# Moving the last eight V matmul groups of a decode attention kernel behind all transposes and scores

## The chip, the cores and the metric

The kernel runs on one core of a Trainium2 chip. The metric is device time in microseconds (us), as a median of several executions. The executions of one kernel still spread by 0.8 to 16 us, and differences of 2 us are what this study is about; so each ratio is between runs of the same rounds on the same chip, and where two kernels of different chips are set side by side, the text says so.

PE is the matmul engine (TensorE), DVE the vector engine, ACT the scalar engine; SP issues the loads. The tiles that the PE writes here (kst, sps, acc in the profiles) are in PSUM. In this kernel an engine waits for another's work, or for a load, by a semaphore.

## The reference, cut to what matters

One query token, 16 query heads of width 256, 8 key/value heads, a cache of 65,536 positions in bfloat16. For each key/value head, two query heads share it:

```
q      = x @ wq                                   # 16 heads x 256
scores = q . K^T * 256**-0.5                      # K: 8 x 65536 x 256
p      = softmax(scores)
o      = p . V                                    # V: 8 x 65536 x 256
a      = o @ wo
out    = g * a + (1 - g) * b                      # b: a small token MLP, g: a gate
```

K and V together are 537 MB, and each element is used once or twice. So the loads matter, and in this kernel the PE loads every 128x128 block of V, and of K transposed, as weights (8192 weight loads of each in the page).

## The kernel before

The cache is cut into 256 chunks of 2048 positions; a load brings four chunks of K or of V (4 MB) into one of five ring slots. I call the last loads K62, K63, V62, V63 (chunks 248 to 251 are in K62 and V62, 252 to 255 in K63 and V63). For a chunk the PE does 32 transposes of K, 32 score matmuls, one matmul that sums the probabilities (denominator) and 32 V matmuls. DVE and ACT copy the transposes out of PSUM, ACT takes the exponential.

```python
    DC = 4          # chunks per load
    NS = 5          # ring slots
    KTB = 2
    PTB = 4         # ring of probability tiles
    LAG = 2
    loads = [(w, cd) for cd in range(NCD) for w in "kv"]
    loads[-3], loads[-2] = loads[-2], loads[-3]        # ..., K62, K63, V62, V63
    # the last load comes in four pieces:
    pieces = [(0, 32), (32, 48), (48, 56), (56, 64)]
    # ... cut ...
            def load(i):                               # SP queue
                w, cd = loads[i]
                slot = i % NS
                # ... cut: wait until the slot's last user on the PE is done ...
                if i < len(loads) - 1:
                    eng.dma_start(ring[:, slot].rearrange("p n d -> p (n d)"), cache_src(w, cd)
                                  ).then_inc(sem_in[slot], 16)
                    return
                # ... cut: the pieces ...

            # PE
            def denominators(c):
                g, k = divmod(c, NCPH)
                pe.wait_ge(sem_exp, c + 1)
                if k == 0 and g >= 1:
                    pe.wait_ge(s_run, g if g >= 2 else 1)
                pe.matmul(acc[:, g % 2, DENC:DENC + 2 * NT], ones_sq[:, :], pT[:, c % PTB, :],
                          start=(k == 0), stop=(k == NCPH - 1))

            def values(c):
                g, k = divmod(c, NCPH)
                cd, cv = divmod(c, DC)
                slot, landed = slot_of("v", cd)
                if cd < NCD - 1 and cv == 0:
                    pe.wait_ge(sem_in[slot], landed)
                # ... cut: 32 matmuls, weights = V block, moving = two columns of pT ...
                ins.then_inc(sem_pv, 1)

            for s in range(NC + LAG):
                if s < NC:
                    transposes(s)
                # ... cut: the projection of q at s == 1 ...
                if 0 <= s - 1 < NC:
                    scores(s - 1)
                if 0 <= s - 2 < NC:
                    denominators(s - 2)
                if 0 <= s - LAG < NC:
                    values(s - LAG)
                # ... cut: mixer and projection of finished heads ...
            project(H - 1)

            # ACT
            def weights(c):
                act.wait_ge(sem_qk, c + 1)
                if c >= PTB:
                    act.wait_ge(sem_pv, c - PTB + 1)
                act.activation(pT[:, c % PTB, :], sps[:, c % 2, 0:2 * NT], AF.Exp, scale=scale
                               ).then_inc(sem_exp, 1)
```

The softmax here doesn't subtract the row's maximum and nothing guards it: scores larger than these inputs give would overflow.

## Time and profile before

| | before |
|---|---|
| time, median of 3 (range) | 1322.87 us (1322.7 to 1323.07) |
| span of the profiled execution | 1319.0 us (its time was 1320.84 us, 2 us under the median) |
| cache bytes, mean rate | 544 MB, 415 GB/s |
| PE busy | 1130.7 us (86%) |

The last line becomes important later: 197 packets brought 3.23 MB of instructions.

The timeline of the PE in before, at the gap that the change is aimed at (start, duration, then line, operation, tiles, count; in brackets the idle time before it and what ended it). `kst<-ident,ring` are the transposes of K, `sps<-qT,ktT` the scores, `acc<-pT,ones_sq` the denominator, `acc<-pT,ring` the V matmuls:

```profile
1282.94 2.37 PE L259 MATMUL kst<-ident,ring 128*128 128x128 bf16 x22 [0.55 <-issue]
1285.10 1.04 PE L275 MATMUL sps<-qT,ktT 128*128 128x2 bf16 x32
1286.00 0.19 PE L286 MATMUL acc<-pT,ones_sq 128*128 128x32 bf16 x1
1292.10 1.02 PE L303 MATMUL acc<-pT,ring 128*128 128x2 bf16 x32 [5.91 <-DMA ring<-in_A_v_cache_dram]
1292.98 3.57 PE L259 MATMUL kst<-ident,ring 128*128 128x128 bf16 x32
```

The PE has done transposes up to chunk 250 and comes to the V matmuls of chunk 248, whose data (V62) has not landed. It sits idle for 5.9 us, although K63, loaded ahead of V62, should be there at about 1280 us (an estimate: it was issued at 1249.4 us, and a load of K takes 29.9 us in the median).

The chain of waits of before, in order of time (start, length, what):

```profile
1261.21 30.84 DMA ring<-in_A_v_cache_dram
1292.05 0.04 issue
1292.10 1.02 PE acc L303 x32
1293.11 3.44 PE kst L259 x32
...
1301.59 1.81 PE kst L259 x32
1303.40 0.78 PE sps L275 x32
...
1313.50 0.82 PE acc L303 x32
```

From V62's landing to the last V matmul there is PE work alone. The transposes of a chunk take 3.44 us when the clock is at half (granted 0.50 from 1293.0 to 1296.6 us) and 1.81 us at full (1.00 from 1298 to 1304 us).

And the waits of the PE over the whole span in before (total, times, longest):

```profile
PE acc L303 <- issue: 54.6, 47, 3.2
PE sps L275 <- issue: 43.0, 35, 2.7
PE kst L259 <- DMA ring<-in_A_k_cache_dram: 36.5, 24, 3.4
PE kst L259 <- issue: 21.6, 24, 2.3
```

"Issue" is idle time for which the profile knows no waker.

### The profile page before, as it was taken

Reading aid. Unit: us, or ns where it says so; the run is one execution under the profiler, and the core shown is the slowest. Engines: PE = TensorE matmul, PEld = TensorE weight load, DVE = VectorE, ACT = ScalarE, POOL = GpSimd, SP = SyncE. Lnnn points to the kernel's source line nnn. Section 1 sums busy time; section 2 is a strip of 40 time slices with the busy share of each in tenths; the row PEclk is TensorE's granted clock in tenths of the full one; section 3 lists DMA queues with packets and bytes.
Section 4 is the critical chain, followed back from the end, with each engine's and each line's share of the span. In section 5 each row is a group of like instructions: output and inputs, shape, how many; then the busy total and the mean of one; then the engine's idle time right before and its main releaser. Section 6 shows DMA issues by size and latency. Waiting matters only on the chain.

```text
span 1319.0 us, 53069 instructions
## 1 busy us (share of the span) xinstructions
PE 1130.7 (86%) x25054; PEld 1104.4 (84%) x25054; DVE 414.1 (31%) x716; ACT 550.2 (42%) x786; POOL 0.9 (0%) x7
## 2 busy tenths in 40 slices
PE   4889888888888888888898889889988888898897
PEld 4888788888888888888888888789888888888896
DVE  3686232222332222222223222222223222232222
ACT  2454343434444434434434444343444344344443
POOL 0000000000000000000000000000000000000000
PEclk9688787777777768778778777786778676777777
DMA  9999999999999999999999999999999999999992
GB/s 400 433 421 430 430 427 431 424 428 428 426 430 428 426 428 427 427 425 408 432 417 431 425 413 427 423 395 428 432 425 429 422 423 420 416 418 427 422 410 97
DMA packets 21560, 547.63 MB, mean 415 GB/s; under 512 B 2265, under 2 KB 4316, under 8 KB 4703
## 3 DMA queue, kind: packets, MB, share of 16 engines
q1 hardware_dynamic: 21330, 544.22, 97.0%
q8 instruction: 197, 3.23, 1.0%
q14 instruction: 21, 0.16, 0.0%
q10 hardware_dynamic: 12, 0.01, 0.0%
HBM read 544.22 MB, written 0.00 MB: 413 GB/s over the span
## 4 chain that ended last, share of the span: by engine, by line
PE 52%; DMA 40%; issue 6%; DVE 1%; ACT 0%; DVEq 0%; SPq 0%; ACTq 0%
DMA ring<-in_A_k_cache_dram 38%; PE kst L259 31%; PE acc L303 10%; PE sps L275 9%; DMA ring<-in_A_v_cache_dram 2%; PE acc L286 0%; PE acc L315 0%; ACT ktT L547 0%; DVE ktT L484 0%; DVEq L449 0%; DVE zring L437 0%; DVE wtmp L435 0%; DVE zring L441 0%; DVE gu L455 0%; SPq L205 0%
## 5 line engine op out<-in xcount | busy, mean ns | idle before, releaser
L547 ACT ACTIVATE ktT<-kst 128x1024 bf16<-128x1024 bf16 x512 | 513.4, 1023 | 699.9 <-PE kst L259 699.6
L259 PE MATMUL kst<-ident,ring 128*128 128x128 bf16 x8192 | 707.8, 265 | 63.0 <-DMA ring<-in_A_k_cache_dram 36.5
L259 PEld LDWEIGHTS kst<-ident,ring 128*128 128x128 bf16 x8192 | 654.1, 122 | 76.4 <-DMA ring<-in_A_k_cache_dram 42.1
L484 DVE COPY ktT<-kst 128x1024 bf16<-128x1024 bf16 x512 | 352.8, 691 | 866.2 <-PE kst L259 853.5
L303 PE MATMUL acc<-pT,ring 128*128 128x2 bf16 x8192 | 251.7, 164 | 61.0 <-issue 54.6
L275 PE MATMUL sps<-qT,ktT 128*128 128x2 bf16 x8192 | 255.0, 164 | 43.1 <-issue 43.0
L275 PEld LDWEIGHTS sps<-qT,ktT 128*128 128x128 bf16 x8192 | 248.5, 99 | 47.6 <-issue 45.8
L303 PEld LDWEIGHTS acc<-pT,ring 128*128 128x128 bf16 x8192 | 231.5, 99 | 66.6 <-issue 60.6
L538 ACT ACTIVATE pT<-sps 128x32 bf16<-128x32 f32 x256 | 50.0, 195 | 43.1 <-PE sps L275 42.9
L286 PE MATMUL acc<-pT,ones_sq 128*128 128x32 bf16 x256 | 45.9, 179 | 1.6 <-issue 1.6
L286 PEld LDWEIGHTS acc<-pT,ones_sq 128*128 128x128 bf16 x256 | 25.1, 98 | 0.0
L338 PE MATMUL acc<-ones_sq,ktT 1*128 1x1 bf16 x28 | 0.9, 161 | 13.5 <-DMA b_b<-in_B_b_dram 13.5
L338 PEld LDWEIGHTS acc<-ones_sq,ktT 1*128 1x128 bf16 x28 | 0.8, 99 | 13.5 <-DMA b_b<-in_B_b_dram 13.5
L315 PE MATMUL acc<-wo_sb,oTn 128*1 128x448 bf16 x32 | 10.7, 473 | 0.8 <-DVE oTn L461 0.8
L532 ACT ACTIVATE zring<-zring 128x448 bf16<-128x448 bf16 x14 | 8.1, 578 | 3.4 <-DVE zring L443 3.4
L437 DVE TENSOR_TENSOR zring<-wtmp,uring 128x448 bf16<-128x448 bf16 x14 | 5.5, 393 | 1.5 <-issue 0.5
L435 DVE TENSOR_TENSOR wtmp<-uring 128x448 bf16<-128x448 bf16 x14 | 5.5, 392 | 1.2 <-issue 0.2
L455 DVE TENSOR_TENSOR gu<-wtmp,zring 128x448 bf16<-128x448 bf16 x14 | 5.5, 392 | 1.0
L441 DVE TENSOR_TENSOR zring<-uring,wtmp 128x448 bf16<-128x448 bf16 x14 | 5.5, 392 | 1.0
L524 ACT ACTIVATE statb<-statb 1x1 bf16<-1x1 bf16 x1 | 0.2, 204 | 13.2 <-DVE statb L407 13.2
L315 PEld LDWEIGHTS acc<-wo_sb,oTn 128*1 128x1 bf16 x32 | 2.4, 92 | 3.8 <-issue 2.0
L323 PE MATMUL acc<-gu,w2p_b 128*1 128x448 bf16 x14 | 5.3, 376 | 0.0
(66 smaller groups left out, 63.6 us busy)
## 6 DMA issues: line engine op xcount, KB each, us to landing
ring<-in_A_k_cache_dram SPq DMA_DIRECT2D x64, 4096.0 KB, 29.9
ring<-in_A_v_cache_dram SPq DMA_DIRECT2D x63, 4096.0 KB, 32.6
wo_sb<-in_A_wo_dram SPq DMA_DIRECT2D x8, 448.0 KB, 30.6
ring<-in_A_wq_dram SPq DMA_DIRECT2D x1, 3072.0 KB, 19.4
ring<-in_A_v_cache_dram SPq DMA_DIRECT2D x1, 2048.0 KB, 27.1
ring<-in_A_v_cache_dram SPq DMA_DIRECT2D x1, 1024.0 KB, 30.2
ring<-in_A_v_cache_dram SPq DMA_DIRECT2D x2, 512.0 KB, 31.4
ring<-in_A_wq_dram SPq DMA_DIRECT2D x1, 512.0 KB, 20.2
```

The source lines that it names most:

```text
L259: ins = pe.transpose(kst[:, b, j * P:(j + 1) * P], ring[:, slot, ck * NT + 4 * b + ntl, dh * P:(dh + 1) * P], ident[:, :])
L275: ins = pe.matmul(sps[:, c % 2, 2 * nt:2 * nt + 2], ktT[:, slot, b, j * P:(j + 1) * P], qT[:, dh, REP * g:REP * g + REP], start=(dh == 0), ...
L286: pe.matmul(acc[:, g % 2, DENC:DENC + 2 * NT], ones_sq[:, :], pT[:, c % PTB, :], start=(k == 0), stop=(k == NCPH - 1))
L303: ins = pe.matmul(acc[:, g % 2, col:col + REP], ring[:, slot, n, dj:DH:2], pT[:, c % PTB, 2 * nt:2 * nt + 2], start=False, stop=(k == NCPH ...
L315: ins = pe.matmul(acc[0:1, g % 2, PRC:PRC + DM], oTn[:, g % 2, dj * REP + hh:dj * REP + hh + 1], wo_sb[:, g % 2, hh, dj * DM:(dj + 1) * DM ...
L435: vec.tensor_tensor(W, U, U, op=ALU.mult)
L437: vec.tensor_tensor(Z, W, U, op=ALU.mult)
L441: vec.tensor_tensor(Z, U, W, op=ALU.add)
L484: vec.tensor_copy(ktT[:, c % KTB, b, :], kst[:, b, :]).then_inc(sem_evd, 1)
L532: act.activation(zring[:, slot, :], zring[:, slot, :], AF.Tanh).then_inc(s_tanh, 1)
L538: act.activation(pT[:, c % PTB, :], sps[:, c % 2, 0:2 * NT], AF.Exp, scale=scale).then_inc(sem_exp, 1)
L547: act.activation(ktT[:, c % KTB, b, :], kst[:, b, :], AF.Copy).then_inc(sem_eva, 1)
```

## The change

The PE asks for V62 before the transposes of chunk 251 and of all of K63. The change moves the V matmuls of the last eight chunks behind everything else, so the PE can use the time in which V62 is on its way. Eight probability tiles then wait for their use, so their ring grows from four to ten. No instruction is added or removed.

```diff
-    PTB = 4
+    PTB = 10
     LAG = 2
-    assert T % (CH * DC) == 0 and NCD > NS
+
+    LATE = 2 * DC
+    assert T % (CH * DC) == 0 and NCD > NS and PTB >= LATE + 2
@@
-                if 0 <= s - LAG < NC:
+                if 0 <= s - LAG < NC - LATE:
                     values(s - LAG)
@@
                 if r == NCPH - 1 and 0 <= g < H - 1:
                     project(g)
+            for c in range(NC - LATE, NC):
+                values(c)
             project(H - 1)
```

## The prediction

> **What bounds the kernel now.** The page shows DMA busy at 90% or more in all but the last of 40 slices (the cache queue 97.0%), PE 86%. The loads bound the kernel until its end; the change touches neither them nor the freeing of their slots before that, so I look at the last 50 us. There the loads are K62, K63, V62, V63, but the PE's program order asks for V62 (values of chunk 248) before the transposes of chunk 251 and of all of K63.
>
> The timeline shows transposes, scores and denominators through 1286.2 us; then PE idle 5.9 us, released by the V load (the only such wait in the last 100 us); V62 lands at 1292.05. From 1292.10 the chain of waits is PE work alone, 22.2 us to 1314.33: eight values, five chunks of transposes, six of scores; then 4.7 us for division, projection, last add and store. V63's pieces land by about 1302 (issued 1269.8 to 1271.1, plus the listed 27.1 to 31.7 us).
>
> **What the change does.** It adds and removes no instruction; it moves eight groups of 32 V matmuls (0.79 us each in the chain of waits, clock full) behind everything else. K63, issued at about 1249.4, lands some 30 us later, at 1280, so the transposes of 251 to 255 and the scores can run through the gap. After them (five chunks at 1.81 + 0.82 us, and one score) V62 and V63 have nearly landed, and the values run as one burst. The ring of ten holds the eight waiting tiles; a depth of four delayed nothing.
>
> **Sum.** Gain: the 5.9 us wait, not the 12 us between V63's landing and the last value, because the PE then works without pause from 1286 to its end. Costs: the last denominator now waits for the last exp (about 0.4 us, was hidden behind values); "issue" gaps of 0.6 to 1.6 us, seen every 10 to 15 us, have no wait to hide in (about 0.6); in the burst of two-column matmuls the clock probably halves, 0.86 instead of 0.79 us per chunk (about 0.4). Possible extra: in windows of 1 us the clock falls to 0.50 at 1283.2 and returns at 1296.8, four times 3.41 us later[...]. Transposes of chunk 251 take 3.44 us at half clock against 1.81. Without the idle stretch the clock may return earlier in the work, worth 0 to 1.6 us; I count 0.8.
>
> 5.9 − 0.4 − 0.6 − 0.4 + 0.8 = 5.3 us, 0.4%. Evictions stay off the limit: per chunk ACT needs 2.15 us, DVE 1.5, PE 2.6.
>
> **Predicted time:** 1317.5 us, 80% range 1315.0 to 1320.2. Faster by over 2%: 0.01; within 2%: 0.98; slower: 0.01.
>
> **What would show it.** Right: no PE wait for V62; transposes of K63 right after 1286; PE nearly without gaps to about 1309; the last 256 V matmuls one block of 6.3 to 7 us; span about 1314. Wrong: a wait for K63 before its transposes; a wait for V63's pieces in the burst (loads bound the end, gain up to 12 us); half clock through the transposes (gain near 3 us); longer gaps from evictions or issue.
>
> **What would make it wrong.** The 5.9 us are one execution's: the PE's lead over V62 hangs on clock phases between 1272 and 1286 us, which the wait now absorbs and later would not, about 2 us each way. The loads may end earlier or later.

The half clock in the burst (0.4) and the earlier return of the clock (0.8) were my estimates, from before: a V group took 0.86 us at a granted 0.50 (from 1265.46 to 1266.32 us) and 0.79 in the chain at 1.00, and 0.8 is half of the difference between 3.44 and 1.81. What was measured of them stands under "The clock" near the end.

## More of the kernel before

All loops are unrolled: the PE executes 25,054 pairs of a weight load and a matmul.

The page of before: busy time of the PE, then the slices (each digit a fortieth of the span, in tenths; PEclk is the granted PE clock), then two of the DMA queues with packets, MB and their share of the 16 engines' time.

```profile
span 1319.0 us, 53069 instructions
...
PE 1130.7 (86%) x25054; PEld 1104.4 (84%) x25054; DVE 414.1 (31%) x716; ACT 550.2 (42%) x786; POOL 0.9 (0%) x7
...
PEclk9688787777777768778778777786778676777777
DMA  9999999999999999999999999999999999999992
...
q1 hardware_dynamic: 21330, 544.22, 97.0%
q8 instruction: 197, 3.23, 1.0%
```

The cache queue keeps the engines busy until the last slice, and the PE has little to spare.

## The result, and the profile after

| | before | after |
|---|---|---|
| time, median of 4 (range) | 1322.97 us (1322.7 to 1323.46) | 1321.33 us (1318.47 to 1322.84) |
| span of the profiled execution | 1319.0 us | 1316.7 us |
| last V matmul group ends | 1314.33 us | 1311.96 us |

The ratio is 0.9985, with a 95% interval of 0.9967 to 1.0002. (A ratio is the mean time of one kernel's fast runs over that of the other's of the same rounds, so it isn't quite the ratio of the medians.) The kernel is about 2 us faster, which this set alone does not tell from noise; that is not the 5.3 us that were forecast; the median lies above the stated range. The profiled execution of after is the fastest of its four (1318.47 us). The executions of after spread over 4.4 us and those of before over 0.8 in these rounds (in later rounds both spread more).

The page of after, the same lines:

```profile
span 1316.7 us, 53063 instructions
...
PE 1125.9 (86%) x25054; PEld 1098.6 (83%) x25054; DVE 413.8 (31%) x716; ACT 549.1 (42%) x786; POOL 0.9 (0%) x7
...
PEclk9788877787886878777677686677677686887878
DMA  9999999999999999999999999999999999999992
...
q1 hardware_dynamic: 21330, 544.22, 97.1%
q8 instruction: 197, 3.23, 1.0%
```

Nothing has changed at this scale. The timeline of the PE in after, from the point at which before sat idle:

```profile
1285.52 1.95 PE L261 MATMUL kst<-ident,ring 128*128 128x128 bf16 x32
...
1288.13 0.49 PE L261 MATMUL kst<-ident,ring 128*128 128x128 bf16 x6
1290.01 1.61 PE L261 MATMUL kst<-ident,ring 128*128 128x128 bf16 x26 [1.38 <-issue]
...
1296.88 1.78 PE L261 MATMUL kst<-ident,ring 128*128 128x128 bf16 x29 [1.66 <-issue]
...
1303.11 0.95 PE L277 MATMUL sps<-qT,ktT 128*128 128x2 bf16 x32 [1.02 <-issue]
```

The wait for V62 is gone, and the transposes of chunk 251 begin at once, at full clock (granted 1.00 from 1281.3 to 1305.2 us), as hoped. But three new idle stretches cut into this work. The first two lie in the middle of a chunk, between the sixth and the seventh transpose or the third and the fourth, where no semaphore is waited for. The third lies before the scores of the last chunk. These wait for the last copy out of PSUM, which ended on ACT at 1302.42 us, 0.33 us into the stretch; the rest of it has no waker.

The chain of waits of after, over the same end:

```profile
1288.63 1.38 issue
...
1295.22 1.66 issue
...
1302.09 1.02 issue
...
1304.54 5.88 PE acc L305 x222
1310.43 0.45 issue
1310.88 1.08 PE acc L305 x34
```

The fourth stretch is in the block of V matmuls at the end (the burst). Together the four are 4.51 us.

The waits of the PE over the whole span in after:

```profile
PE acc L305 <- issue: 56.3, 52, 2.6
PE sps L277 <- issue: 49.3, 39, 2.7
PE kst L261 <- issue: 33.0, 27, 2.9
PE kst L261 <- DMA ring<-in_A_k_cache_dram: 29.7, 23, 3.3
```

The issue waits have grown to 138.6 us. In before there is none at all between 1286 us and the last V matmul.

**What the stretches are.** I counted PE matmuls in the trace. The stretches follow matmuls 24,506, 24,633, 24,760 and 25,016: distances of 127, 127 and 2 x 128. Earlier stretches lie on the same grid and often at the same matmuls in both kernels (22,853, 23,362, 23,744 and 23,998, for example). A pair is two instructions, so the grid is one of 256 instructions. The trace shows a queue (q8) that brings instructions: 197 packets of 16,384 bytes, and 50,108 weight loads and matmuls are 195.7 blocks of 256. So I count one packet as a block of 256 PE instructions. And the four stretches end 1.37 to 1.47 us after such a packet has ended. The same holds over the whole span: of 130 gaps of over 0.5 us between matmul starts in before, 101 end 1.1 to 1.75 us after an instruction packet (after: 115 of 142). So at these places the PE has run out of instructions. Nor does it seem to have more than about one block ahead: in the 5.9 us of idle time of before only one packet came, at 1287.4 us, and the next started 10.6 us later.

Over the whole span these packets start 6.26 us (before) and 6.43 us (after) apart in the median, mostly between 6.0 and 7.5. That alone says little, as 197 packets in 1319 us are 6.7 us apart on average whatever limits them; but between two blocks in succession that the PE stood waiting for, the median is 6.37 us (38 pairs, before) and 6.76 us (55 pairs, after). At the end of after they start at 1287.6, 1294.4, 1300.6, 1304.4, 1308.5 and 1312.2 us: 6 to 7 us apart while the cache loads run, about 4 us apart as these run out (from 1299 to 1303.5 us the cache queue is down to 28% of the 16 engines, and its last packet ends at 1302.7 us). In before it is 3.6 to 4.7 us from 1298.0 us on (its last cache packet ends at 1302.4 us). The 4 us are partly the PE's own pace in the burst, so the supply may be faster still. At full clock a chunk of transposes and scores is 2.6 us for 130 instructions, so 256 instructions last 5.1 us. That is less than the 6 to 7 us that the next block takes to come.

This is the supply theory: while the loads run, the PE gets 256 instructions per 6 to 7 us whatever it could do, so PE work moved forward from the time after V62's landing into the time of the loads is worth only part of its length. Its rivals are the clock theory (the gain is lost to a half clock) and the landing theory (V63's pieces end the kernel).

### The profile page after: what moved, and what is told of

It reads as the page before. It is cut to its first block, busy times and chain, and to the rows that moved or that the text cites. A ratio compares the mean times of both kernels' runs of the same rounds, so it can differ in the third digit from the quotient of the medians.

```text
span 1316.7 us, 53063 instructions
## 1 busy us (share of the span) xinstructions
PE 1125.9 (86%) x25054; PEld 1098.6 (83%) x25054; DVE 413.8 (31%) x716; ACT 549.1 (42%) x786; POOL 0.9 (0%) x7
## 3 DMA queue, kind: packets, MB, share of 16 engines
q1 hardware_dynamic: 21330, 544.22, 97.1%
## 4 chain that ended last, share of the span: by engine, by line
PE 60%; DMA 31%; issue 8%; DVE 0%; ACT 0%; ACTq 0%; DVEq 0%
PE kst L261 36%; DMA ring<-in_A_k_cache_dram 30%; PE acc L305 11%; PE sps L277 11%; DMA b_b<-in_B_b_dram 1%; PE acc L288 1%; PE acc L317 1%; PE acc L325 0%; PE sps L356 0%; DVE ktT L488 0%; ACT L529 0%; PE sps L358 0%; DVE out_b L479 0%; DVE stat L409 0%; ACTq L521 0%
## 5 line engine op out<-in xcount | busy, mean ns | idle before, releaser
L261 PEld LDWEIGHTS kst<-ident,ring 128*128 128x128 bf16 x8192 | 647.3, 122 | 79.4 <-issue 45.2
```

The costliest lines, as they stand in the source:

```text
L261: ins = pe.transpose(kst[:, b, j * P:(j + 1) * P], ring[:, slot, ck * NT + 4 * b + ntl, dh * P:(dh + 1) * P], ident[:, :])
```

## The experiments

All ratios are against the kernel before, in the same rounds. "Arrival" is the time at which the PE gets to chunk 251's transposes in the new orders, or to the V matmuls of chunk 248 in the old one, in the profiled execution.

| run | chip | this, median us (range) | before, median us | ratio (95%) |
|---|---|---|---|---|
| after_again | 1 | 1322.27 (1317.92 to 1324.41) | 1323.2 | 0.9983 (0.9960 to 1.0006) |
| skip_tail_loads | 1 | 1319.66 (1314.65 to 1322.77) | 1323.2 | 0.9967 (0.9943 to 0.9991) |
| half_packets_after | 1 | 1326.08 (1325.23 to 1326.90) | 1323.2 | 1.0015 (0.9995 to 1.0035) |
| half_packets_before | 1 | 1331.24 (1330.48 to 1331.73) | 1323.2 | 1.0054 (1.0033 to 1.0076) |
| before_again | 12 | 1324.91 (1320.22 to 1327.87) | 1322.76 | 0.9994 (0.9956 to 1.0033) |
| wait_put_back | 12 | 1324.18 (1322.89 to 1330.54) | 1322.76 | 1.0003 (0.9962 to 1.0044) |
| values_four_behind | 12 | 1320.44 (1317.70 to 1324.16) | 1322.76 | 0.9964 (0.9928 to 1.0000) |
| skip_tail_before | 12 | 1317.81 (1312.20 to 1321.46) | 1322.76 | 0.9945 (0.9906 to 0.9984) |
| fewer_sums_new_order | 8 | 1319.69 (1319.32 to 1320.34) | 1322.76 | 0.9978 (0.9965 to 0.9992) |
| fewer_sums_old_order | 8 | 1323.03 (1322.55 to 1324.06) | 1322.76 | 1.0004 (0.9989 to 1.0020) |
| values_four_behind_again | 8 | 1321.87 (1318.87 to 1329.98) | 1322.76 | 1.0002 (0.9977 to 1.0027) |
| after_third | 8 | 1321.13 (1317.55 to 1322.71) | 1322.76 | 0.9985 (0.9969 to 1.0002) |
| sums_old | 2 | 1322.64 (1321.94 to 1328.49) | 1323.04 | 0.9999 (0.9974 to 1.0024) |
| sums_changed | 2 | 1318.79 (1316.98 to 1327.55) | 1323.04 | 0.9974 (0.9947 to 1.0001) |
| sums_changed_skip | 2 | 1318.34 (1314.54 to 1320.96) | 1323.04 | 0.9956 (0.9934 to 0.9978) |
| sums_old_skip | 2 | 1315.97 (1312.29 to 1319.48) | 1323.04 | 0.9941 (0.9918 to 0.9965) |

Before itself spread from 1320.66 to 1336.6 us over the four later chips, with medians of 1322.76 to 1323.2.

### The changed kernel again, twice

No edit.

> The changed kernel, unedited, for a second profile and more times. Supply theory: the PE gets its instructions in blocks of 256 (127 or 128 weight-load and matmul pairs), and while the cache loads run a block comes only every 6.1 to 7.2 us, so work moved forward into the loads' time starves; expected again three to five idle stretches without a named waker at block boundaries after the K62 landing, together 3 to 5 us, and a ratio to before of 0.997 to 1.000. Clock theory (the gain is lost to half clock in the transposes of the last chunks): half clock through most of the last 30 us and few such stretches. Landing theory (the V63 pieces end it): a wait for V in the burst.

> Third set of the changed kernel, beside the others on one chip: ratio to before 0.9975 to 0.9995; in its profile the transposes of chunk 251 begin between 1285 and 1293 us, and the earlier they begin, the more idle time at block boundaries follows.

The ratios are 0.9983 and 0.9985: with the first set, three sets agree on 2.0 to 2.2 us, though each interval alone touches 1. The profile of after_third repeats that of after: arrival at 1285.4 us, three stretches (1.10, 1.66 and 1.02 us) at the same matmuls. The profile of after_again is different:

```profile
1291.76 3.48 PE L261 MATMUL kst<-ident,ring 128*128 128x128 bf16 x32
...
1295.90 1.95 PE L261 MATMUL kst<-ident,ring 128*128 128x128 bf16 x32
...
1307.22 0.94 PE L277 MATMUL sps<-qT,ktT 128*128 128x2 bf16 x32 [0.42 <-issue]
```

Here the PE arrived at 1291.8 us, six microseconds later, with chunk 251 at half clock (by the 3.48 us of its transposes), and only one stretch of 0.42 us follows. That one is no block boundary: the last copy out of PSUM ends on ACT at 1307.12 us, and the scores of chunk 255, which wait for it, start 0.10 us later (the same 0.10 us in skip_tail_loads and skip_look2). In the old order the V matmuls of chunk 253 stand at this place and hide the copy; the new order lays it bare. There would have been no wait for V62 to remove: in the profiles of the old order it lands at 1292.0 to 1293. So this expectation (three to five stretches) was missed, and it showed that the arrival itself varies from one execution to another. In neither is there a wait for V in the burst: the landing theory falls.

### The kernel before again

No edit.

> The kernel before, unedited, against itself: the noise of this comparison, and a second profile of its end. Ratio 1.000, interval at most 0.002 to each side. If the 5.9 us wait for V62 in the first profile was typical, the wait is 5 to 7 us here as well; if it hangs on how far the PE happens to lag behind the loads (the transposes of chunk 251 began at 1285.5, 1290.9 and 1291.8 us in three profiles of kernels with the same program up to there), it is anything from 0 to 7 us, and the mean gain of the reordering is smaller than the 5.9 us for this reason too.

The comparison of before with itself gave 0.9994, with an interval of 0.004 to each side, twice as wide as expected: 2 us can't be told apart in one such set. Its profile has the wait for V62:

```profile
1290.13 0.94 PE L275 MATMUL sps<-qT,ktT 128*128 128x2 bf16 x32
1290.93 0.18 PE L286 MATMUL acc<-pT,ones_sq 128*128 128x32 bf16 x1
1292.56 0.98 PE L303 MATMUL acc<-pT,ring 128*128 128x2 bf16 x32 [1.45 <-DMA ring<-in_A_v_cache_dram]
```

It is 1.45 us and not 5.91, because the PE came later. The last V matmul ended 0.5 us after that of the first profile all the same: in the old order V62's landing sets the end, and the arrival hardly shows.

### The tail loads left out

Edit (wrong result on purpose; both orders):

```diff
-                slot, landed = slot_of("v", cd)
-                if cd < NCD - 1 and cv == 0:
+                slot, landed = slot_of("v", min(cd, NCD - 3))
+                if cd < NCD - 2 and cv == 0:
@@ (the waits for the four pieces are removed)
-            for i in range(1, len(loads)):
+            for i in range(1, len(loads) - 2):
```

> The changed kernel without the loads of V62 and V63; their matmuls read V61's data instead (wrong result on purpose), same instructions on the PE. The DMA queues are empty from about 1284 us. Supply theory: the blocks then come every 3.7 to 4.1 us and the idle stretches at block boundaries shrink from 4.5 us to under 1.5 us in sum; the end comes 3 to 4 us before that of the changed kernel (about 0.3%). Clock theory: no change, within 1 us, as the PE work is the same. Landing theory: the end moves forward only if a wait for V was in the burst, and there was none: no change.

> The kernel before without the loads of V62 and V63 (their matmuls read V61's data, wrong result on purpose): the wait for V62 goes, the order stays, and the loads are gone after about 1284 us. Supply theory: the wait's removal is now paid in full; the PE goes through chunk 251 to the end at about 3.4 us a chunk without idle stretches, and the time is 4 to 7 us below before, within 1.5 us of the changed kernel without these loads. Clock theory (the idle stretch helped the PE's clock): the time is no more than 2 us below before.

With the changed order the time fell by 2.6 us against after_again (medians, same chip), a little less than the 3 to 4 that were expected; with spreads of 6.5 and 8.1 us in six executions each, this isn't clear of noise. In the profile only the 0.42 us of the last copy are left from chunk 251 to the last V matmul, and the chunks run at an even 2.6 us. The blocks then come no faster than the PE uses them up (5.0 to 6.9 us apart from 1287 to 1306 us), so the expected 3.7 to 4.1 us couldn't show. But the PE arrived late (1290.9 us), so this profile alone doesn't tell the absence of the loads from a late arrival. With the old order the time fell by 5 us (ratio 0.9945), within the 4 to 7 expected, and there is no idle stretch at all. So removing the wait and the loads together pays about what the wait was long; the clock theory expected at most 2 us, and the interval (2.1 to 12.4 us) only just excludes that.

The two differ by 1.85 us in the medians, on different chips, in favour of the old order, which the noise of six executions each does not confirm. The profiles do show a price of the new order itself. From chunk 251 to the last V matmul the old order took 19.6 us and the new one 21.7, of which 0.8 us is the V group of chunk 248 that the old order does before. The rest is 1.3 us; I put it down to the last exponential, now exposed (0.25 us), the last copy (0.42 us), and the burst of two-column matmuls (6.93 us in the timeline), at half clock by the measure of after (granted 0.50 from 1305.2 to 1312 us).

### Loads in halves

```diff
+    LP = 2
@@
-            return i % NS, 16 * (i // NS + 1)
+            return i % NS, 16 * LP * (i // NS + 1)
@@
-                    eng.dma_start(ring[:, slot].rearrange("p n d -> p (n d)"), cache_src(w, cd)
-                                  ).then_inc(sem_in[slot], 16)
+                    for n0 in range(0, DC * NT, DC * NT // LP):
+                        n1 = n0 + DC * NT // LP
+                        eng.dma_start(ring[:, slot, n0:n1, :].rearrange("p n d -> p (n d)"),
+                                      cache_src(w, cd, n0, n1)).then_inc(sem_in[slot], 16)
```

> The changed kernel with every cache load cut into two loads of half the rows, so the pieces that each DMA engine takes are 16 KB instead of 32 KB; same bytes, same order, same PE instructions. Supply theory: an instruction block waits behind four or five pieces of 1.21 us; with pieces of half the length the spacing of the blocks falls from 6.2 to 7.2 us to about 4 us, idle stretches at block boundaries mostly vanish in the whole span (from about 135 us to under 50 us in sum), and the end comes 3 to 6 us earlier than in the changed kernel. If a block waits behind an amount of bytes rather than of pieces, nothing changes. Clock and landing theories: no change beyond 1 us.

> The kernel before with the same cut of the loads. Supply theory: the idle stretches vanish as well, but the end hangs on V62's landing (about 1292) plus 22 us of PE work, so the time falls by less than 2 us. Then the reordering is worth 5 to 8 us once the supply is out of the way (half_packets_after against this one). Clock theory: the reordering is worth the same 0 to 3 us with either cut.

Both expectations on the time failed. The instruction packets are 6.44 us apart in the median, as with whole loads (6.43), and between two blocks in succession that the PE stood waiting for, 6.30 us (22 pairs; 6.76 in after). So a block does not wait behind a fixed number of pieces; about 4 us were expected. The issue waits fell to 86.1 us in sum, not under 50, and the time went into waits for K. Both kernels became slower, by 3.8 us (half_packets_after against after_again) and 8.0 us (half_packets_before against before), because the loads did (by their pages the packets of the cache queue took 97.5% of 1325.1 us and 97.2% of 1329.5 us, 1292 us in both; in after and before it was 97.1% of 1316.7 and 97.0% of 1319.0, about 1279 us). The profiles show the PE waiting for K far longer than in after (29.7 us). In half_packets_after:

```profile
PE kst L264 <- DMA ring<-in_A_k_cache_dram: 113.7, 56, 5.5
PE acc L308 <- issue: 34.9, 30, 2.1
PE sps L280 <- issue: 32.2, 27, 2.0
PE kst L264 <- issue: 19.0, 23, 1.7
```

The pair is useful all the same. With slower loads the PE is ahead of them at the end (a wait for V62 of 6.7 us in half_packets_before), and the reordering is worth 5.2 us: 1331.24 against 1326.08, on the same chip, with spreads of 1.3 and 1.7 us. That is what I had forecast for the kernel as it is, and within the 5 to 8 us expected here, but by luck: the blocks came no faster, and the profile of half_packets_after still has 2.6 us of issue stretches after its arrival (1.66, 0.67 and 0.30 us). The gain came from a longer wait for V62 to remove. So what the change gains depends on how far the PE is ahead of the loads when it gets to V62.

### The wait put back

```diff
+                if s == NC - LATE + 3:
+                    pe.wait_ge(sem_in[slot_of("v", NCD - 2)[0]], slot_of("v", NCD - 2)[1])
                 if s < NC:
                     transposes(s)
```

> The changed kernel, but the PE waits for V62's landing before the transposes of chunk 251; the V matmuls stay in one block at the end. Supply theory: the PE works off the rest after the wait, while the loads drain, so instruction blocks come in time: idle stretches at block boundaries after the wait under 1 us in sum, and the time is that of the kernel before plus 0.5 to 1.5 us (last exp exposed, half clock in the burst). If the stretches came from the new order itself (the burst, or chunks without values in between), they stay at about 4 us and the time is 3 us or more above before.

The ratio is 1.0003, the forecast +0.5 to +1.5 us within a wide interval (0.008). In its profile the PE arrived at 1293.9 us, after V62, so the wait didn't happen, and stretches of 1.10 us (at a block boundary) and 0.43 us (the last copy) followed, where under 1 us was expected. This run is inconclusive: it fits the theory in the time and tests little in the profile.

### The values four steps behind

Edit against the changed kernel: instead of one block, each late group follows four steps behind its transposes.

```diff
+                if NC - LATE <= s - LAG - 2 < NC:
+                    values(s - LAG - 2)
@@
-            for c in range(NC - LATE, NC):
+            for c in range(NC - 2, NC):
                 values(c)
```

> The changed kernel with the last eight value groups not in one block but four steps behind their transposes (two steps more than elsewhere): V62's matmuls begin after the transposes of chunk 252. No wait for V62 remains, the last exp is hidden again and the clock has transposes between the values. Supply theory: idle stretches at block boundaries as in the changed kernel up to about 1302 us, less after; 0.5 to 1.5 us faster than the changed kernel in the end, ratio to before about 0.998. If the single block at the end was the cost, the gain rises to 4 us or more, ratio under 0.997.

> Repeat of the version with the values four behind, for more times: ratio to before 0.996 to 0.998, that is 3 to 5 us; and 0 to 2 us under the changed kernel.

The two sets gave 0.9964 and 1.0002, with intervals that touch 1: inconclusive. The first set alone met the sign named for the block at the end as the cost (a ratio under 0.997); the repeat did not. The profiles show what they should: no wait for V62 and none for the last exponential. The first arrived late (1293.6 us), had one stretch of 0.27 us and took 20.8 us to the last V matmul. The second arrived early (1286.0 us), had stretches of 3.2 us in sum and took 26.4 us, part of it at half clock (from 1292.4 to 1299.3 us).

### Fewer instructions on the PE

One denominator matmul of 128 columns for four chunks instead of one for each: 184 pairs, 368 instructions, fewer. In the old order, in the order with values four behind, and (in the second set) in the changed order; the ring of probability tiles has 12 places in all of them.

```diff
                 pe.wait_ge(sem_exp, c + 1)
+                if k % DG != DG - 1 and k != 0:
+                    return
@@
-                pe.matmul(acc[:, g % 2, DENC:DENC + 2 * NT], ones_sq[:, :], pT[:, c % PTB, :],
-                          start=(k == 0), stop=(k == NCPH - 1))
+                n = 1 if k == 0 else DG - 1 if k == DG - 1 else DG
+                c0 = c - n + 1
+                col = DENC + 2 * NT * (c0 % DG)
+                pe.matmul(acc[:, g % 2, col:col + 2 * NT * n], ones_sq[:, :],
+                          pT[:, c0 % PTB:c0 % PTB + n, :].rearrange("p a b -> p (a b)"),
+                          start=(k == 0), stop=(k == NCPH - 1), skip_group_check=True)
```

> The version with the values four behind, and in addition one denominator matmul for four chunks (128 columns) instead of one a chunk: 184 of 25,054 weight-load and matmul pairs fewer, 368 instructions, 1.44 blocks of 256. Ring of 12 tiles. Supply theory: at 6.6 us a block while loads run, the PE gains up to 9.5 us on the loads over the span, so it is ahead of the loads at the end more often; the time falls by 2 to 7 us against before (the loads, which end near 1302 us, and the work after them set the floor). If the loads alone set the pace until the end, the time falls by less than 3 us.

> The order of the kernel before with the same cut of denominator matmuls. Supply theory: the PE is further ahead at the end, so the wait for V62 comes back in full (4 us or more in its profile, against 1.6 us in the second profile of before), the time falls by only 0 to 3 us, and the new order is worth 3 to 6 us on top of it. If the new order's worth doesn't hang on the PE's lead, it is worth the same 2 us as without the cut.

The old order with fewer instructions is not faster (1.0004): the end still hangs on V62. Its profile has a wait for V62 of 3.6 us, a little less than the 4 expected. The new order is faster than before (0.9978, interval below 1), and between the two lie 3.3 us (1323.03 against 1319.69), with spreads of only 1.0 and 1.5 us. In the profile of the new order the PE arrived at 1287.4 us and lost 3.0 us in stretches. This is the version whose lead over before is clearest, 2.9 us; against the changed kernel of the same rounds (1321.13) its lead of 1.4 us is not clear of noise.

The second set, with the tail loads left out in both orders as well:

> Old order, fewer denominator matmuls, again, for a comparison on one chip: 1322.5 to 1324 us, a wait for V62 of 3 to 7 us in the profile, no idle stretch at a block boundary after it.

> The changed order (all late values in one block at the end), fewer denominator matmuls. Both the supply and the clock theory: no wait for V62. Supply theory: 2 to 5 us of idle stretches at block boundaries between chunk 251 and 1303 us, and a time 2 to 4 us below the old order. If the prediction's sum held once the PE is ahead of the loads, the time is 5 us or more below.

> The changed order, fewer denominator matmuls, V62 and V63 not loaded (V61's data read instead, wrong result on purpose). Supply theory: the stretches at block boundaries after 1285 us fall under 1 us, and the time falls 2.5 to 4.5 us against the changed order with these loads. If the stretches have nothing to do with the loads, they stay and the time changes by less than 1 us.

> The old order, fewer denominator matmuls, V62 and V63 not loaded. Supply theory: with both the wait and the competing loads gone the time falls by 5 to 8 us against the old order with these loads, to within 1.5 us of the changed order without them: the order alone is then worth nothing. If the order itself has a worth apart from the wait, it stays.

The wait for V62 was 5.4 us in the profile of sums_old. The changed order is 3.9 us faster in the medians (1322.64 against 1318.79), within the 2 to 4 expected (3.1 in the means, not clear of noise); one of its six executions took 1327.55, and it was the profiled one: the PE was late at chunk 248 already (1285.4 us) and arrived at 1298.0. With the loads left out, the old order fell by 6.7 us (expected: 5 to 8). The changed order fell by only 0.5 us in the medians, where 2.5 to 4.5 were expected: a miss, though the means fell by 2.4 us and the noise allows either. Its profile has no stretch at a block boundary any more, but again a late arrival (1292.3 us). (The scores of the last chunk still wait 0.62 us there; the profile puts that down to ACT and not to issue.) The old order without the loads is 2.4 us faster in the medians than the changed one without them, not within 1.5 us. That again isn't clear of noise (1.9 us in the means), but it has the sign of a new order that costs more than the 0.8 us of the prediction (0.4 and 0.4).

### Two more looks without the tail loads

> A second look at the changed kernel without the loads of V62 and V63 (wrong result on purpose). Supply theory: whatever the arrival, the stretches at block boundaries from chunk 251 to the last V matmul stay under 1 us in sum and that part takes 21 to 23.3 us (23.3 if the transposes of chunk 251 run at half clock). If the stretches belong to an early arrival and not to the loads, an arrival before 1288 us shows 3 us or more of them and 25 us or more.

> The same with fewer denominator matmuls, a second look: same numbers, 21 to 23 us from chunk 251 to the last V matmul whatever the arrival.

Single executions of 1317.94 and 1318.31 us, beside 1320.86 for before. The PE timeline of skip_look2:

```profile
1289.25 1.95 PE L261 MATMUL kst<-ident,ring 128*128 128x128 bf16 x32
...
1291.87 1.95 PE L261 MATMUL kst<-ident,ring 128*128 128x128 bf16 x32
...
1302.89 0.94 PE L277 MATMUL sps<-qT,ktT 128*128 128x2 bf16 x32 [0.42 <-issue]
```

From chunk 251 to the burst it runs at full clock, as after and after_third did (1.95 us for 32 transposes in all three, and in after the granted clock was 1.00), and up to the last V matmul it loses 0.59 us to issue (0.42 of it the last copy) instead of 4.5 and 3.8. It took 22.0 us to the last V matmul (sums_skip_look2: 21.9), as expected. The arrivals were 1289.3 and 1289.7 us, not below 1288, so the strictest form of the test did not come up.

All profiles of the new orders side by side (issue: idle stretches marked so in the timeline between arrival and last V matmul; the length is to the start of the last V matmul):

| loads | profile | arrival, us | arrival to last V, us | issue, us | last V, us |
|---|---|---|---|---|---|
| all | after_third | 1285.4 | 25.4 | 3.8 | 1310.9 |
| all | after | 1285.5 | 26.3 | 4.5 | 1311.8 |
| all | values_four_behind_again | 1286.0 | 26.4 | 3.2 | 1312.4 |
| all | fewer_sums_new_order | 1287.4 | 25.2 | 3.0 | 1312.5 |
| all | after_again | 1291.8 | 23.6 | 0.4 | 1315.3 |
| all | values_four_behind | 1293.6 | 20.8 | 0.3 | 1314.4 |
| all | wait_put_back | 1293.9 | 23.2 | 1.5 | 1317.2 |
| without V62, V63 | skip_look2 | 1289.3 | 22.0 | 0.6 | 1311.3 |
| without V62, V63 | sums_skip_look2 | 1289.7 | 21.9 | 0.0 | 1311.5 |
| without V62, V63 | skip_tail_loads | 1290.9 | 21.7 | 0.4 | 1312.5 |
| without V62, V63 | sums_changed_skip | 1292.3 | 21.9 | 0.0 | 1314.2 |

In the profiles with the V block at the end, 0.42 us of the issue column is the last copy; the sums rows have 0.62 us there that the profile puts down to ACT.

(sums_changed, at 1298.0 us, and half_packets_after, with slower loads, are left out; they took 22.7 and 25.7 us.) With all loads, the four early profiles arrive at 1286.1 us on average and the three late ones at 1293.1, 7.0 us later; their last V matmuls are at 1311.9 and 1315.6 us, only 3.7 us apart. (These are four and three executions, and of different kernels.) Most of the rest goes into stretches at block boundaries; in values_four_behind_again some goes into half clock (1292.4 to 1299.3 us), and in fewer_sums_new_order, which without its stretches took 22.2 us against 20.5 in values_four_behind, I put some down to it too. At full clock the PE has 5.1 us of work per block against a block every 6 to 7 us; after a late arrival it does more of its work after the loads have ended, when blocks come about every 4 us (3.7 to 4.1 in after). Without the loads every profile took 21.7 to 22.0 us, so within these arrivals (1289.3 to 1292.3 us) an earlier one is paid in full.

## Why the prediction was wrong

**The place and the mechanism** were right: the wait for V62 vanishes, K63's transposes move into it, no wait for V63 replaces it, and the end is PE work.

**The step that failed first** is the term "'issue' gaps of 0.6 to 1.6 us, seen every 10 to 15 us, have no wait to hide in (about 0.6)". Measured: 4.5 us in the profile of after and 3.8 us in after_third. I counted the gaps at the rate of the kernel's mixed clock (0.76 on average in before); and at that rate the 23 us of work should have had about two, where 0.6 us is one small one. At full clock the PE uses up a block of 256 instructions in 5.1 us, and while the loads run the next one takes 6 to 7; so there is a gap at every block, of 1 to 1.7 us. (Of the third gap, 0.42 us would be there without it: the last copy, a cost that the prediction did not list. That leaves 4.1 and 3.4 us for the blocks.) The sum for the profile of after is then 5.9 us (wait) − 4.5 (issue) − 0.25 (last exponential; 0.4 forecast) − 0.4 (burst: 6.96 us in the chain for eight groups, against 6.6 in before) + 1.6 (chunk 251 at full clock, 1.81 for 3.44; 0.8 forecast) = 2.4 us. The last V matmul did end 2.4 us earlier (1314.33 to 1311.96); a few tenths each way are left out.

**The second step** is the wait itself: "Gain: the 5.9 us wait". It was one execution's, as the prediction says under what would make it wrong. Profiles of the old order with whole loads show 5.9, 1.45, 5.4 and 3.6 us, and of the seven profiles of new orders in the table with all loads three arrived at about V62's landing or after it, so had little or nothing to gain. There the new order only costs: the last V matmul of after_again and wait_put_back is at 1315.3 and 1317.2 us, later than the 1314.1 and 1314.7 of the two profiles of before. (wait_put_back arrived at 1293.9 us, so part of its delay is the arrival.) So in the few profiles there are, the changed kernel's last V matmul ends 2.4 to 3.8 us earlier with an early arrival and no earlier with a late one, which fits its mean gain of 2.0 us. The range of the prediction allowed 2 us for the arrival, but 6 to 8 us are seen.

**The premise** "The loads bound the kernel until its end" was too simple. The loads are busy 97% of the time, but the PE of before also idles 119 us with no known waker, mostly at block boundaries, against 36.5 us for K: the two run about level, and which is ahead at the end changes from one execution to the next. Where the loads are made slower (half packets), the PE is ahead and the change is worth 5.2 us.

**The clock** was not the loss: after and after_third ran at full clock from chunk 251 to the burst (granted 1.00 until 1305.2 us in after; 1.95 us for 32 transposes in both) and stood still anyway. The burst fell to half clock as predicted (0.50 from 1305.2 to 1312 us in after), at the cost predicted (0.4 us). In both traces the granted clock is either 0.50 or 1.00, and it changes in steps of 3.41 us. How busy the PE is does not settle it: from 1306 to 1310 us of after, in the burst, the PE is busy 4.00 of the 4 us (by the profile, which models the ends of matmuls) at a clock of 0.50; from 1308 to 1312 us of before, with transposes among the work, the same 4.00 of 4 us have 1.00. That the clock returns earlier without the idle stretch was not shown: in after it was back at 1.00 at 1281.3 us, before the two orders part at 1285.5 us.

**What stays open.** That the running loads slow the instruction blocks is supported by their spacing within one trace (6 to 7 us, then about 4) and by four profiles without the tail loads, all four at full clock from chunk 251 to the burst by their 1.95 us for 32 transposes, as after was, and with no stretch of over 0.2 us at a block boundary; an arrival as early as 1285 us without these loads never came up, and the times alone don't show it clear of noise (2.6 us by skip_tail_loads, 0.5 by sums_changed_skip). One spacing speaks against it: in before a block started 3.7 us after that of 1298.0 us, with the DMA engines at 0.46 to 0.51 until 1301 us. Why a block needs 6 to 7 us beside the loads isn't known. It is not the number of pieces ahead of it, and it does not follow the total load: from 1286 to 1300 us of after the DMA engines are only about half busy (0.43 to 0.53 of the 16, in stretches of 2 us), and the blocks are still 6.8 and 6.2 us apart. Why the PE's arrival varies by 8 us is not settled either.

## What to carry to other kernels

A wait in one profile is worth its length only if other executions have it and if the work that moves into it can run at the rate you have measured elsewhere; look at both before you add up. When a fully unrolled kernel shows idle time marked as issue, count the instructions between the gaps: a fixed distance of about 256, with an instruction packet that ended 1.37 to 1.47 us before each restart, was the sign here that the engine was out of instructions. Fewer instructions are then worth a try, though 368 fewer gave nothing in the old order here (1.0004 and 0.9999) and no lead over the changed kernel that is clear of noise. A change that takes away a wait for the slowest stream can hand the end over to the next one, here the instruction supply of the PE.
